# Top-k attention and an MLP on one core: GpSimd's sums in two set places of a step, with a third buffer, and earlier copies in the last two steps

## The chip, the core and the metric

The kernel runs on one core of a Trainium2 chip. A core has five engines that run side by side, each through its own list of instructions in order: TensorE (PE, matmuls; PEld is its loading of weights), VectorE (DVE), ScalarE (ACT), GpSimd (POOL) and SyncE (SP, which here only issues DMAs). They wait for each other through semaphores. The metric is the device time of one launch in microseconds (us); lower is better.

## The reference, cut to what matters

```python
def _attn_ref(q, k, v):                       # 8 batches, 8 heads, 576 rows, 64 columns
    scores = np.matmul(q, k.transpose(0, 1, 3, 2)) / np.sqrt(D)
    kth = np.partition(scores, -32, axis=-1)[..., -32:-31]
    scores = np.where(scores >= kth, scores, -1e9)
    scores = scores - np.max(scores, axis=-1, keepdims=True)
    attn = np.exp(scores)
    attn = attn / (np.sum(attn, axis=-1, keepdims=True) + 1e-09)
    return np.matmul(attn, v)

def _moe_ref(x, w_in, w_out):                 # x 4608x512, w_in 512x2048, w_out 2048x512
    h = x @ w_in
    neg, pos = h <= -1.0, h >= 1.0
    g = np.where(pos, h, np.where(neg, 0.0, (h + 1.0) ** 2 / 4.0))
    return g @ w_out
```

Between the two, the attention output of all heads of a row becomes one row of `x`. So each row of scores keeps its 32 largest entries, and the MLP's activation is zero, a parabola or the identity.

## The kernel before

**Steps and chunks.** The attention is done in 144 steps (`steps`), each with two tiles of 128 rows of scores with 576 columns. Four steps give the 128 rows of `x` of one chunk; there are 36 chunks, and `mlp` puts the MLP of a chunk into a list, `pending`, as soon as its attention is done.

**VectorE in a step.** `weights` finds the 32nd largest of each row. `pairs` (L381) makes `more` and `less`, the larger and the smaller of columns j and j+288. MAX8 takes eight largest entries at a time, and MATCH_REPLACE8 (L388) removes them. A scan (L460) merges the two lists into the threshold `kth`, and L467 multiplies `e`, the exponentials, by the mask, and sums them up. VectorE then takes the reciprocal `rz` (L413).

**Dividing and turning the weights.** `divide` has GpSimd multiply `e` by `rz` (L420, two instructions a step, and a small one, `excess`, L423). `move_w` has ScalarE copy `e` into two halves of 16 bits (`halves`, L497, one buffer), SP write them to DRAM (`rows`), and SP read them back transposed into `wT` by a DMA (L296), issued in a later place through `reads_of_rows`. `values` multiplies `wT` by v on TensorE (`po`, L514 and L522), and ScalarE copies the result into `xT`. In the first eight steps, while weights of the MLP are still converted (`early`), TensorE transposes instead and the halves aren't used.

**The MLP of a chunk.** `hidden` multiplies a group of 256 hidden units (`ph`, L547; 8 groups a chunk). `read` has ScalarE make `r` and `g` from it (L558, L566). `bound` has GpSimd bound `r` to at most 1, square it, and add it to `g` (L573, L575, L576): these are GpSimd's sums. `final` multiplies 128 hidden units of `g` by `w_out` into `py` (L586). The finals of a group are listed four groups (`LAG`) behind its `hidden`. After the last final, ScalarE copies `py`, which has one buffer, to `y` (L589). The very last chunk is cut finer, takes its sums on VectorE, and has its finals in halves (`py_half`, L600).

**The order of the work.** It is written out by hand: all engines run in the order in which the main loop emits. A step m has seven slots. In slot 0 `weights` emits two MAX8 with `divide` of step m-1, and two MATCH_REPLACE8; in slot 1 two more of each; in slot 3 `more` of step m+1, `less` of step m, and the first MAX8 of step m+1 with its first `exp`; in slot 4 the second `exp`; in slot 5 the rest, up to L467. `move_w` of step m-1 stands in slot 3. In slot 2 of every even step stand the scores (`sp`, L367) of two steps and the `values` of two. In each slot, `advance` emits as much of `pending` as the estimated TensorE time allows.

**GpSimd's sums before.** `read` appends a `bound` to the list `bounds`, with the number of the slot. It is emitted when the next `read` finds more than one in the list, when a final needs it, or at the end of the slot two or more after its own. `r` has two buffers, so ScalarE's read of a group waits until the sums of the group two before it are done.

Of the kernel before, what the change touches and what calls it, by code (L numbers as in the profile page):

```python
# [11 lines left out]
F32 = mybir.dt.float32  # L12
# [5 lines left out]
ALU = mybir.AluOpType  # L18
# [8 lines left out]
def kernel(  # L27
# [10 lines left out]
    nc = tc.nc  # L38
    B, H, S, D = q.shape
    NTOK, DM = out.shape  # L40
    DFF = moe_w_in.shape[1]
    P = 128
# [8 lines left out]
    SH = S // 2  # L51
# [4 lines left out]
    GROUP = 2  # L56
# [120 lines left out]
    def run(ctx, paired):  # L177
# [197 lines left out]

        def pairs(st, op, name, bufs):
            s = st["s"]
            st[name] = x = att.tile([P, 2, SH], F32, name=name, bufs=bufs)  # L380
            nc.vector.tensor_tensor(out=x, in0=s[:, :, 0:SH], in1=s[:, :, SH:S], op=op)  # L381

        def largest(st, r):
            return [partial(nc.vector.max, out=eight(st["tops"], i, r), in_=st["rest"][:, i, :]) for i in range(2)]
# [6 lines left out]
        def first_top(st, between=None):  # L391
            s, e = st["s"], st["e"]
            if paired:
                pairs(st, ALU.max, "more", 2)
            if between is not None and paired:
                pairs(between, ALU.min, "less", 1)
            st["rest"] = st["more"] if paired else s
            st["tops"] = tops = att.tile([P, 2 * TOP_K], F32, name="tops", bufs=3)
            nmax = att.tile([P, 2], F32, name="nmax")
            for x in largest(st, 0):  # L400
                x()  # L401
            nc.scalar.activation(nmax, tops[:, 0:2 * SPLIT:SPLIT], AF.Copy, scale=-1.0)
            for i in range(2):
                nc.scalar.activation(e[:, i, :], s[:, i, :], AF.Exp, bias=nmax[:, i:i + 1])  # L404
                yield
# [132 lines left out]
        def mlp(xT, rows, pool, last):  # L538
            gs, group, whole_g = {}, 1 if last else GROUP, set()
            py = []  # L540

            def hidden(x):
                ph = ps.tile([P, group, P], F32, name="ph", tag="ph", bufs=3)
                for i in range(group):
                    f = x * group + i
                    for kk in range(NK):
                        nc.tensor.matmul(ph[:, i], w_in[:, kk, f * P:(f + 1) * P], xT[:, kk],  # L547
                                         start=(kk == 0), stop=(kk == NK - 1))

                reads.append(partial(read, x, ph))  # L550
                if not holding:
                    issue_reads()

            def read(x, ph):
                while len(bounds) > 1:
                    bounds.popleft()[1]()
                r = pool.tile([P, GROUP, P], F32, name="r", bufs=2)[:, 0:group]
                nc.scalar.activation(r, ph, AF.Relu, bias=half, scale=0.5 * unit)  # L558
                gs[x] = g = pool.tile([P, GROUP, P], F32, name="g", bufs=2 * LAG)[:, 0:group]
                if last:  # L560
                    nc.scalar.activation(g, ph, AF.Relu, bias=minus_half, scale=0.5 * unit)
                    nc.vector.scalar_tensor_tensor(out=r, in0=r, scalar=1.0, in1=r, op0=ALU.min, op1=ALU.mult)
                    nc.vector.tensor_tensor(out=g, in0=r, in1=g, op=ALU.add)
                    whole_g.add(x)
                    return
                nc.scalar.activation(g, ph, AF.Relu, bias=minus, scale=unit)  # L566
                by_act = converted < n_pieces and x % 2
                if by_act:
                    nc.scalar.activation(r, r, AF.Square)
                bounds.append((slots_done, partial(bound, x, r, g, by_act)))  # L570

            def bound(x, r, g, by_act):
                nc.gpsimd.tensor_scalar(r, r, 1.0, 0.0, ALU.min, ALU.max)  # L573
                if not by_act:
                    nc.gpsimd.tensor_tensor(out=r, in0=r, in1=r, op=ALU.mult)  # L575
                nc.gpsimd.tensor_tensor(out=g, in0=r, in1=g, op=ALU.add)  # L576
                whole_g.add(x)

            def final(f):
                if f == 0:  # L580
                    py.append(ps.tile([P, DM], F32, name="py", tag="py", bufs=1))
                if f // group not in gs:
                    issue_reads()
                while f // group not in whole_g:
                    bounds.popleft()[1]()
                nc.tensor.matmul(py[0], gs[f // group][:, f % group], w_out[:, f, :], start=(f == 0), stop=(f == NF - 1))  # L586
                if f == NF - 1:
                    y = (late or words).tile([P, DM], F32, name="y", bufs=1)
                    nc.scalar.activation(y, py[0], AF.Copy, scale=unit)  # L589
                    for p0, p1, dst in rows:  # L590
                        nc.sync.dma_start(out=dst, in_=y[p0:p1])

            HALF = DM // 2

            def final_half(f, c):
                if f == 0:
                    py.append(ps.tile([P, HALF], F32, name="py_half", tag="a" if c else "py", bufs=2 if c else 1))
                nc.tensor.matmul(py[c], gs[f][:, 0], w_out[:, f, c * HALF:(c + 1) * HALF], start=(f == 0), stop=(f == NF - 1))  # L600

            def final_halves(f):
                for c in range(2):
                    final_half(f, c)

            def last_finals():
                for c in range(2):
                    for f in range(NF - LAG, NF):
                        final_half(f, c)
                    y = late.tile([P, HALF], F32, name="y_half", tag="y", bufs=1) if c else \  # L610
                        pool.tile([P, HALF], F32, name="y_first", tag="r", bufs=2)
                    nc.scalar.activation(y, py[c], AF.Copy, scale=unit)
                    for p0, p1, dst in rows:
                        nc.sync.dma_start(out=dst[:, c * HALF:(c + 1) * HALF], in_=y[p0:p1])

            behind = []
            while pending and pending[-1][3]:
                behind.insert(0, pending.pop())
            for x in range(NF // group + LAG):
                if last and x == 0:  # L620
                    for _ in range(2):
                        pending.append(behind.pop(0)[0:3] + (False,))
                if x < NF // group:
                    pending.append((NK * group, needed(x * group + group - 1, False), partial(hidden, x), False))
                if x < LAG:
                    for _ in range(min(GROUP + 1, len(behind))):
                        pending.append(behind.pop(0)[0:3] + (False,))
                elif last:
                    if x < NF:
                        pending.append((DM // P, needed(x - LAG, True), partial(final_halves, x - LAG), True))  # L630
                    elif x == NF:
                        pending.append((LAG * DM // P, needed(NF - 1, True), partial(last_finals), True))
                else:
                    for f in range((x - LAG) * group, (x - LAG + 1) * group):
                        pending.append((DM // P, needed(f, True), partial(final, f), x >= NF // group))
# [14 lines left out]
        n = len(steps)  # L650
# [8 lines left out]
        converted, inspected, due = 0, 0, 0.0  # L659

        reads, bounds, holding, slots_done = [], deque(), False, 0

        def issue_reads():
            while reads:
                reads.pop(0)()
# [75 lines left out]
        state = []  # L741
# [41 lines left out]
        for _ in first_top(state[0]):  # L783
            pass
# [19 lines left out]
        for m in range(n + 2):  # L804
            early = converted < n_pieces
# [21 lines left out]
            for slot in range(SLOTS):  # L827
# [11 lines left out]
                if slot == 1 and 1 <= m <= n and state[m - 1]["by_tensor"]:  # L839
                    pe_time = max(pe_time, done[m - 1] + 2.0) + 1.0  # L840
                    transpose_w(state[m - 1])
                    ready_at[m - 1] = pe_time + 1.8
                if slot == 3 and 1 <= m <= n and state[m - 1] is not None and not state[m - 1]["by_tensor"]:
                    move_w(state[m - 1])
                    ready_at[m - 1] = done[m - 1] + 15.0
                if slot == 1 and late is not None and paired and m % 2 == 0:
# [47 lines left out]
                        nc.tensor.transpose(rest[:, i % NT, :], ident, ident)  # L894
                advance((EARLY_SHARE if early else share) / SLOTS if m < n - 2 else 32.0, now)
                slots_done += 1
                while bounds and (early or m >= n or bounds[0][0] < slots_done - 2):
                    bounds.popleft()[1]()
            for _ in (top_k if top_k is not None else ()):
                pass  # L900
        while pending:
            advance(32.0, pe_time + 8.0)
            while bounds:
                bounds.popleft()[1]()
        order.__exit__(None, None, None)


# [45 lines left out]
```

## Time and profile before

| what | before |
|---|---|
| median of 3 runs | 1471.42 us (1471.32 to 1472.72) |
| the profiled execution | 1469.45 us, of which span 1467.6 |
| PE busy | 1430.7 us (97%) |
| DVE busy | 1396.8 us (95%) |
| ACT busy | 1161.1 us (79%) |
| POOL busy | 928.5 us (63%) |
| chain that ended last | PE 78%, DVE 14%, ACT 4%, DMA 2%, issue 2% |

A span goes from the first to the last instruction. Busy time is the union of an engine's instructions. The chain that ended last is followed back from the last instruction to whatever released it, step by step. A group of instructions is named by its line, engine and operation, and by what it writes and reads. A wait is idle time of an engine just before an instruction, and is put down to what came last.

### The profile page before, as it was taken

Reading aid. Unit: us, or ns where it says so; the run is one execution under the profiler, and the core shown is the slowest. Engines: PE = TensorE matmul, PEld = TensorE weight load, DVE = VectorE, ACT = ScalarE, POOL = GpSimd, SP = SyncE. Lnnn points to the kernel's source line nnn. Section 1 sums busy time; section 2 is a strip of 40 time slices with the busy share of each in tenths; the row PEclk is TensorE's granted clock in tenths of the full one; section 3 lists DMA queues with packets and bytes.
Section 4 is the critical chain, followed back from the end, with each engine's and each line's share of the span. In section 5 each row is a group of like instructions: output and inputs, shape, how many; then the busy total and the mean of one; then the engine's idle time right before and its main releaser. Section 6 shows DMA issues by size and latency. Waiting matters only on the chain.

```text
span 1467.6 us, 31975 instructions
## 1 busy us (share of the span) xinstructions
PE 1430.7 (97%) x10731; PEld 1045.9 (71%) x10731; DVE 1396.8 (95%) x4392; ACT 1161.1 (79%) x2216; POOL 928.5 (63%) x1314
## 2 busy tenths in 40 slices
PE   7998899999999999999999999999999999999998
PEld 5766577777777777777777777777777777777677
DVE  6989999999999999999999999999999999999932
ACT  6986878888778888887778887888778888777643
POOL 3473576667666666666666666666666666676640
PEclk7999999999999999999999999999999999999999
DMA  7642767886668886987667986887668886665430
GB/s 240 194 133 64 189 180 196 218 206 172 173 171 212 217 206 178 221 216 178 167 172 201 216 213 173 219 225 184 159 168 199 218 212 175 171 172 153 137 105 18
DMA packets 517919, 264.87 MB, mean 180 GB/s; under 512 B 467696, under 2 KB 476144, under 8 KB 517744
## 3 DMA queue, kind: packets, MB, share of 16 engines
q1 hardware_dynamic: 517744, 262.73, 68.3%
q8 instruction: 87, 1.43, 0.4%
q14 instruction: 88, 0.72, 0.2%
HBM read 62.39 MB, written 104.86 MB: 114 GB/s over the span
## 4 chain that ended last, share of the span: by engine, by line
PE 78%; DVE 14%; ACT 4%; DMA 2%; issue 2%; SPq 0%; ACTq 0%
PE ph L547 29%; PE py L586 27%; PE sp L367 9%; PE po L514 8%; DVE more L388 3%; DVE e L467 3%; DVE more L381 1%; DVE less L381 1%; DVE tops L429 1%; DVE tops L437 1%; PE pw L482 1%; DVE tops L448 1%; DVE seconds L455 1%; PE po L522 1%; PE py_half L600 1%
## 5 line engine op out<-in xcount | busy, mean ns | idle before, releaser
L547 PEld LDWEIGHTS ph<-xT,w_in 128*128 128x128 f32 x4608 | 547.7, 192 | 97.8 <-issue 66.4
L547 PE MATMUL ph<-xT,w_in 128*128 128x128 f32 x4608 | 556.3, 276 | 2.7 <-ACT g L566 2.1
L586 PE MATMUL py<-w_out,g 128*128 128x512 f32 x1120 | 527.0, 598 | 2.0 <-ACT y L589 2.0
L573 POOL TENSOR_SCALAR r<-r 128x256 f32<-128x256 f32 x280 | 136.2, 487 | 398.2 <-ACT r L558 394.0
L388 DVE MATCH_REPLACE8 more<-tops,more 128x288 f32<-128x288 f32 x864 | 374.7, 437 | 0.0
L420 POOL TENSOR_SCALAR e<-e,rz 128x576 f32<-128x576 f32 x272 | 307.7, 1141 | 11.9 <-DVE rz L413 11.9
L586 PEld LDWEIGHTS py<-w_out,g 128*128 128x128 f32 x1120 | 194.2, 191 | 166.0 <-issue 164.7
L497 ACT COPY halves<-e 128x1152 uint16<-128x1152 uint16 x272 | 297.8, 1142 | 2.0 <-DMA rows<-halves 2.0
L576 POOL TENSOR_TENSOR g<-r,g 128x256 f32<-128x256 f32 x280 | 229.8, 821 | 22.0
L467 DVE SCALAR_TENSOR_TENSOR e<-s,kth,e 128x577 f32<-128x577 f32 x288 | 241.0, 872 | 0.1
L404 ACT ACTIVATE e<-s,nmax 128x576 f32<-128x576 f32 x288 | 222.5, 773 | 4.7
L558 ACT ACTIVATE r<-ph,half 128x256 f32<-128x256 f32 (+1 forms) x296 | 136.6, 462 | 99.5 <-PE ph L547 88.3
L368 ACT ACTIVATE s<-sp 128x576 f32<-128x576 f32 x288 | 171.9, 650 | 37.3 <-PE sp L367 34.6
L575 POOL TENSOR_TENSOR r<-r 128x256 f32<-128x256 f32 x276 | 180.2, 653 | 23.0
L367 PE MATMUL sp<-kT,qT 64*128 64x288 f32 x1024 | 163.1, 436 | 4.8 <-ACT kT L265 3.4
L514 PE MATMUL po<-wT,v_in 128*64 128x128 f32 x2048 | 139.1, 277 | 6.5 <-DMA wT<-rows 6.2
L367 PEld LDWEIGHTS sp<-kT,qT 64*128 64x128 f32 x1024 | 90.3, 189 | 76.2 <-issue 30.8
L381 DVE TENSOR_TENSOR more<-s 128x576 f32<-128x576 f32 x144 | 136.1, 945 | 7.9 <-ACT s L368 7.9
L514 PEld LDWEIGHTS po<-wT,v_in 128*64 128x64 f32 x2048 | 113.9, 137 | 31.7 <-issue 13.0
L566 ACT ACTIVATE g<-ph,minus 128x256 f32<-128x256 f32 x280 | 130.8, 467 | 0.0
L429 DVE MAX8 tops<-more 128x8 f32<-128x288 f32 x288 | 125.3, 442 | 0.0
L401 DVE MAX8 tops<-more 128x8 f32<-128x288 f32 x288 | 116.2, 442 | 0.0
(95 smaller groups left out, 1340.8 us busy)
## 6 DMA issues: line engine op xcount, KB each, us to landing
rows<-halves SPq DMA_DIRECT2D x136, 576.0 KB, 3.2
lines<-parts SPq DMA_DIRECT2D x52, 256.0 KB, 3.4
q_in<-in_q_dram SPq DMA_DIRECT2D x32, 256.0 KB, 4.0
v_in<-in_v_dram SPq DMA_DIRECT2D x32, 256.0 KB, 3.9
raw<-in_moe_w_in_dram SPq DMA_DIRECT2D x32, 256.0 KB, 3.4
raw<-in_moe_w_out_dram SPq DMA_DIRECT2D x32, 256.0 KB, 3.4
out_dram<-y SPq DMA_DIRECT2D x31, 256.0 KB, 3.3
kT<-in_moe_w_in_dram SPq DMA_DIRECT2D x8, 512.0 KB, 4.8
```

Source lines behind the costliest of these rows:

```text
L367: nc.tensor.matmul(*x, start=True, stop=True)
L368: nc.scalar.activation(s[:, :, c0:c1], sp[:, :, 0:SH], AF.Copy, scale=SCALE)
L388: nc.vector.match_replace(out=st["rest"][:, i, :], in_to_replace=eight(st["tops"], i, r - 8), in_values=src[:, i, :], imm_value=LOWEST)
L404: nc.scalar.activation(e[:, i, :], s[:, i, :], AF.Exp, bias=nmax[:, i:i + 1])
L420: nc.gpsimd.tensor_scalar(st["e"][:, i, :], st["e"][:, i, :], rz[:, i:i + 1], 1.0, ALU.mult, ALU.mult)
L467: nc.vector.scalar_tensor_tensor(out=st["all"][1][:, i, :], in0=st["all"][0][:, i, :], scalar=last[i], in1=st["all"][1][:, i, :], op0=ALU. ...
L497: nc.scalar.copy(halves[:, :, i * S:(i + 1) * S], st["e"][:, i, :].bitcast(U16).rearrange("p (k t) -> p t k", t=2))
L514: nc.tensor.matmul(po[j * D:(j + 1) * D], v_in[:, h, c, :] if c < NT else tail_values(v_tl, h, t), wT[:, block(j, c)], start=(c == 0), sto ...
L547: nc.tensor.matmul(ph[:, i], w_in[:, kk, f * P:(f + 1) * P], xT[:, kk], start=(kk == 0), stop=(kk == NK - 1))
L575: nc.gpsimd.tensor_tensor(out=r, in0=r, in1=r, op=ALU.mult)
L576: nc.gpsimd.tensor_tensor(out=g, in0=r, in1=g, op=ALU.add)
L586: nc.tensor.matmul(py[0], gs[f // group][:, f % group], w_out[:, f, :], start=(f == 0), stop=(f == NF - 1))
```

## The change

It does four things. `r` gets a third buffer, and `read` empties `bounds` only when more than two groups stand in it. The three operations of a group become single entries, so that part of a group can be emitted. After the conversion, and before the attention ends, they are emitted in two places: two at the end of slot 0, four at the end of slot 3, and the first of the four waits until VectorE has done `less` (the result of `pairs`, kept in `pairs_done`). And `move_w` stands in slot 1 instead of 3 for the last step but one, and in slot 0 for the last.

```diff
+        pairs_done = None
+
         def pairs(st, op, name, bufs):
...
-            nc.vector.tensor_tensor(out=x, in0=s[:, :, 0:SH], in1=s[:, :, SH:S], op=op)
+            return nc.vector.tensor_tensor(out=x, in0=s[:, :, 0:SH], in1=s[:, :, SH:S], op=op)
...
             if between is not None and paired:
-                pairs(between, ALU.min, "less", 1)
+                nonlocal pairs_done
+                pairs_done = pairs(between, ALU.min, "less", 1)
...
             def read(x, ph):
-                while len(bounds) > 1:
-                    bounds.popleft()[1]()
-                r = pool.tile([P, GROUP, P], F32, name="r", bufs=2)[:, 0:group]
+                while len(bounds) > 2:
+                    bound_some(len(bounds[0]))
+                r = pool.tile([P, GROUP, P], F32, name="r", bufs=3)[:, 0:group]
...
-                bounds.append((slots_done, partial(bound, x, r, g, by_act)))
-
-            def bound(x, r, g, by_act):
-                nc.gpsimd.tensor_scalar(r, r, 1.0, 0.0, ALU.min, ALU.max)
+                work = [partial(nc.gpsimd.tensor_scalar, r, r, 1.0, 0.0, ALU.min, ALU.max)]
                 if not by_act:
-                    nc.gpsimd.tensor_tensor(out=r, in0=r, in1=r, op=ALU.mult)
-                nc.gpsimd.tensor_tensor(out=g, in0=r, in1=g, op=ALU.add)
-                whole_g.add(x)
+                    work.append(partial(nc.gpsimd.tensor_tensor, out=r, in0=r, in1=r, op=ALU.mult))
+
+                def complete():
+                    whole_g.add(x)
+                    return nc.gpsimd.tensor_tensor(out=g, in0=r, in1=g, op=ALU.add)
+
+                work.append(complete)
+                bounds.append(work)
...
                 while f // group not in whole_g:
-                    bounds.popleft()[1]()
+                    bound_some(1)
...
+        def bound_some(amount, behind=None):
+            for _ in range(amount):
+                if not bounds:
+                    break
+                ins = bounds[0].pop(0)()
+                if behind is not None:
+                    tc.add_manual_dep(getattr(ins, "ins", ins), getattr(behind, "ins", behind).name,
+                                      mybir.DependencyInfo(mybir.DependencyClass.Sync, mybir.DependencyReason.ANTI),
+                                      reason="GpSimd's sums stand between VectorE's")
+                    behind = None
+                if not bounds[0]:
+                    bounds.popleft()
...
-                if slot == 3 and 1 <= m <= n and state[m - 1] is not None and not state[m - 1]["by_tensor"]:
+                if slot == (3 if m < n - 1 else n - m) and 1 <= m <= n and state[m - 1] is not None and not state[m - 1]["by_tensor"]:
                     move_w(state[m - 1])
...
                 slots_done += 1
-                while bounds and (early or m >= n or bounds[0][0] < slots_done - 2):
-                    bounds.popleft()[1]()
+                if early or m >= n:
+                    while bounds:
+                        bound_some(1)
+                elif slot == 0:
+                    bound_some(2)
+                elif slot == 3:
+                    bound_some(4, pairs_done)
```

More of the change, by code (lines that the diff above doesn't have):

```diff
@@ L610, in last_finals @@
                     y = late.tile([P, HALF], F32, name="y_half", tag="y", bufs=1) if c else \
-                        pool.tile([P, HALF], F32, name="y_first", tag="r", bufs=2)
+                        pool.tile([P, HALF], F32, name="y_first", tag="r", bufs=3)
                     nc.scalar.activation(y, py[c], AF.Copy, scale=unit)
@@ L903, in run @@
             while bounds:
-                bounds.popleft()[1]()
+                bound_some(1)
         order.__exit__(None, None, None)
```

## The prediction

> **What bounds the kernel now.** I read the page's first two parts, then the table of busy time by stretch, the waits by stretch, the chain of waits, and last the timeline of single engines where those pointed.
>
> The stretches (window, length, then busy us of PE, PEld, DVE, ACT, POOL, the granted clock, DMA share, GB/s):
>
> ```profile
> 182.00:430.00 248.00, 245.23 (x1876) 178.68 (x1877) 248.00 (x782) 200.46 (x384) 165.27 (x230) 1.00 0.72 188
> 430.00:1384.00 954.00, 954.00 (x7237) 693.07 (x7234) 954.00 (x3027) 781.79 (x1480) 647.55 (x913) 1.00 0.74 191
> 1384.00:1421.50 37.50, 37.50 (x259) 26.89 (x257) 22.80 (x70) 20.15 (x37) 24.58 (x41) 1.00 0.46 132
> 1421.50:1430.50 9.00, 6.11 (x46) 4.23 (x46) 0.45 (x2) 0.53 (x2) 0.07 (x1) 0.81 0.32 66
> ```
>
> Two engines are full at once from 430 to 1384, so busy time does not decide. Start-to-start times do. In the TensorE timeline between 805 and 823 us each run begins where the last one's issue ends: 16 `ph` matmuls take 1.79 us, 4 `py` matmuls 1.72 us, and these numbers recur in every period of four steps (37.77 us). No TensorE wait at all is listed between 440 and 1390. VectorE's durations do vary there. In this group table for 440 to 1390 (busy us, mean ns, idle before) the unequal pair is `more` and `less`, the same operation on the same shape:
>
> ```profile
> L467 DVE SCALAR_TENSOR_TENSOR e<-s,kth,e 128x577 f32<-128x577 f32 x202 | 164.4, 849 | 0.0
> L381 DVE TENSOR_TENSOR more<-s 128x576 f32<-128x576 f32 x100 | 97.5, 975 | 0.0
> ...
> L381 DVE TENSOR_TENSOR less<-s 128x576 f32<-128x576 f32 x100 | 74.5, 745 | 0.0
> ```
>
> and on GpSimd's side:
>
> ```profile
> L420 POOL TENSOR_SCALAR e<-e,rz 128x576 f32<-128x576 f32 x200 | 241.6, 1217 | 0.0
> ```
>
> `more` costs 0.23 us more than `less`; L467's shortest is 801 ns against a mean of 849; L420's shortest is 737 against 1217. The two engines block each other. So from 430 on TensorE sets the pace and VectorE's lost time is its slack. Before that it is VectorE: the chain from 380 to 424 us is nearly all DVE, and TensorE waits:
>
> ```profile
> PE py L586 <- ACT y L589: 2.0, 4, 1.3
> PE po L522 <- ACT s L368: 0.6, 1, 0.6
> PE po L514 <- DMA wT<-rows: 0.2, 1, 0.2
> ```
>
> At the end TensorE stands still once more, and restarts slowly (the 40 `po` before took 2.33 us, these last 20 take 2.33 alone):
>
> ```profile
> 1418.11 3.60 PE L586 MATMUL py<-w_out,g 128*128 128x512 f32 x8
> 1421.64 1.09 PE L514 MATMUL po<-wT,v_in 128*64 128x128 f32 x16
> 1422.56 0.39 PE L514 MATMUL po<-wT,v_tail 128*64 128x128 f32 x4
> 1425.84 1.98 PE L514 MATMUL po<-wT,v_in 128*64 128x128 f32 x16 [2.89 <-DMA wT<-rows]
> 1427.54 0.70 PE L514 MATMUL po<-wT,v_tail 128*64 128x128 f32 x4
> 1428.17 0.37 PE L915 MATMUL pworst<-ident,worst 128*1 128x128 f32 x1
> 1428.34 2.36 PE L586 MATMUL py<-w_out,g 128*128 128x512 f32 x4
> 1430.53 1.05 PE L547 MATMUL ph<-xT,w_in 128*128 128x128 f32 x8
> ```
>
> **What the skill says.** The Trainium skill, "SBUF — State Buffer", section "Who interferes with whom": a VectorE operation with two SBUF inputs contends with a GpSimd operation that reads SBUF; the first holds the port for its whole instruction and the other waits; with one input VectorE does not contend. The trace agrees: `more`, `less` and L467 have two inputs and stretch, MAX8 and MATCH_REPLACE8 have one and stay within some ns of 436. "TensorE: Matmul & The Clock Gate", section "What's actually happening": TensorE falls to half clock after idling and needs sustained work to return. The trace agrees at the end: granted clock 0.81 and doubled spacing after the pause at 1423. "Perfetto Trace Analysis", section "Tensor Engine Instruction (MATMUL, LD_WEIGHTS)": matmul ends are a model, which is why I use start to start.
>
> **The change, part by part.**
>
> *GpSimd's sums.* Nothing is added to or removed from any engine but a wait; two groups a step, three operations each, are still six a step, and the change places 2+4. The waiting instruction is the first of the four sums, behind `less`. Queued behind it: the other three sums, and then the next step's two L420; ACT waits for those through `halves`, and for `r` buffers, TensorE for `g`. I check each with the steps whose `rz` start at 764.57 and 774.14.
>
> (a) Slot 0. `rz` ends at 774.28; two L420 at 0.74 each, 0.17 for `excess`, then `r` min 0.48 and square 0.61 end near 777.1. `more` starts at 776.98. All between are one-input operations, so the overlap left is 0.1 to 0.2 us.
> (b) Slot 3. `less` of the first step starts at 768.31, and its successor at 768.98. Four sums of 0.70, 0.48, 0.69 and 0.70 (start to start) end near 771.6; L467 starts at 772.09. They fit.
> (c) So VectorE's step loses about 0.23 + 2x0.05 = 0.33 us of blocking and keeps 0.1 to 0.2: 9.44 becomes some 9.25 us. TensorE's 37.77 per four steps (9.44) does not move. From 430 to 1384 I count nothing: the cover is TensorE's own work.
> (d) Latest reader. Walking the queue, groups read by ACT in a period come to 2, 1, 2, 3 per step and leave no remainder. Tightest: the group read at 767.80 gets min and square in the next step's slot 0, its addition after that step's `less` (778.72), so near 779.5; TensorE's eight `py` from 780.35 need it at the third final, 782.1. Margin 2.5 us. The third `r` buffer frees each at least 4 us ahead of its next writer. Cost nothing; if `less` comes over 2.5 us later against TensorE, a stall per chunk.
> (e) 182 to 430. TensorE's delayed starts there, beyond regular spacing: 1.51 at 195.17, 0.46 at 233.34, 0.85 at 255.64, 0.34 at 293.88, 0.47 at 386.42, 0.48 at 424.67, together 4.1 us. Most is the single `py` waiting for ACT's `y`, which stands behind `exp` and `halves`, and these wait for VectorE. VectorE's blocking in this stretch is 0.41 us a step (`more` 860, `less` 800, L467 919 against 741, 741 and 801), over 26 steps far more than needed, but the stall at 195 comes too soon to go whole. Bounds 0 and 4.1; I take 3.0. What is late next is TensorE.
> (f) Before 182: until 115 the sums are emitted at once in both versions. The stalls from 137 to 161 hang on a chain of ACT copies and two DMAs (`halves` 151.37, `rows` 153.58, `wT` 156.80 to 161.38) that no sum enters. I take 0; -2 to +1.5, since VectorE is full there too.
>
> *The last two steps.* `rz` of the step before last is at 1397.93, but its L420 starts at 1402.08 behind one group of sums; its `halves` only at 1409.00, behind five reads, of which one waited 3.42 us for an `r` buffer. The last step's `rz` is at 1405.82, its L420 at 1411.96 behind three more groups, its `halves` at 1415.14 after 2.04 us of waiting for the single `halves` buffer, still being read by the DMA. Then 2.21 + DMA near 3.2 + transposing DMA 4.69 give 1425.8.
> After: the sums held back let L420 follow `rz` at once, so 1398 to 1399.5, and `halves` in place 1 comes after about three reads, near 1403; its `rows` DMA issues at 1405.5 and lands near 1409. SP's queue takes the `wT` transpose next and then the last `rows`; the `y` write at 1403.87 is short. Last step: L420 behind the four sums of slot 3 and one group that a read flushes, near 1407; `halves` in place 0, ahead of the `xT` copies, near 1409 to 1411; `rows` 1411.3 to 1414.5; `wT` to 1419.2. TensorE asks at 1422.8. Margin 3.6 us, so the wait goes whole. ACT's reads and `xT` copies move back by one or two 2.2 us copies; `ph` has three buffers and the matmuls of 1406.79 need the read of 1402.13, so I charge nothing, at most 1 us.
> Without the wait `po` 1.17, the transpose 0.2 and `py` 1.75 end at 1425.9 instead of 1430.53: 4.6 us, with the slow clock in it. I take 4.5 (bounds 2.5 and 4.8). From there the last chunk runs on TensorE unchanged.
>
> **Sum.** 3.0 + 0 + 4.5 = 7.5 us. The profiled execution took 1469.45 (span 1467.6): it would take 1462.0. The median of the runs is 1.97 us higher, 1471.42, so 1463.9.
>
> **Rivals.**
> A (forecast, 0.62): as above, 1460.5 to 1466.
> B, only the tail or only the middle pays (0.15): 4.5 or 3.0 off, 1466.9 or 1468.4. For it: VectorE is full from 137 to 430, so the `y` waits may shift to another order. Against: they vanish by themselves in the old kernel after 430.
> C, no change (0.07): VectorE's slack is refilled by new collisions and the last `halves` still comes late behind flushed sums; 1470 to 1471.4.
> D, slower (0.10): the four sums that wait for `less` reach the third final of the eight `py` too late. It decides once `less` falls more than 2.5 us back against TensorE. At 0.5 us for each of some 33 chunks that is 16.5 us, less the 4.5 of the tail: 1483. For it: one strict queue with a cross-engine wait. Against: margins in (d), and VectorE gets faster, not slower.
> E, larger gain (0.06): the stalls before 182 shrink too, another 2 to 4 us: 1460.
> That the placing fails to separate the engines would be C; (a) and (b) speak against it.
>
> **The numbers.** Likeliest 1463.9. The range 1459 to 1469.5 takes in A, E and nearly all of B; D, C and scraps of the others stay out. What a measurement here can tell from no change is about 0.2%, 2.9 us, so faster means below 1468.5: A, E and most of B, 0.82. Within 0.2%: C and B's rest, 0.08. Slower: 0.10.
>
> **What would show it.** Mean `more` near 0.80 or below and L420 near 0.75; L467 near 0.81; VectorE with idle time before `more` or on `s` after 430; still no TensorE wait there and the period still 37.77; no `y` waits of TensorE after 233; L420 within 0.2 us behind `rz`; the last `po` without a DMA wait, and the last chunk's first `ph` still 37 us before the end of the span but some 7 us sooner than 1430.5. **What would make it wrong:** a TensorE wait on a GpSimd `g` between 440 and 1390, a changed period, or a last `wT` that lands after TensorE asks.

## The result, and the profile after

The median fell from 1471.42 to 1466.79 us (9 runs each; the changed kernel's lie between 1464.32 and 1468.83). The ratio of the two kernels' times is 0.9965, with a 95% interval of 0.9954 to 0.9975. That is about 5.2 us faster (the medians alone lie 4.6 us apart), where 7.5 were forecast. Each ratio below is to runs of the kernel before that were made alongside, whose median lay between 1469.95 and 1471.42 us, so the ratios can be compared more closely than the times. The profiled execution took 1464.38 us, 5.07 less than that of before.

The page's span and busy times of the changed kernel:

```profile
span 1462.1 us, 32172 instructions
...
PE 1426.9 (98%) x10731; PEld 1043.3 (71%) x10731; DVE 1392.5 (95%) x4392; ACT 1159.5 (79%) x2216; POOL 810.1 (55%) x1314
```

GpSimd was busy 118 us less with the same 1314 instructions: its multiplications no longer wait inside, as the lines below show. VectorE's share has not moved. The stretches (columns as before the change):

```profile
182.00:430.00 248.00, 247.01 (x1893) 180.26 (x1892) 248.00 (x789) 203.12 (x389) 141.56 (x235) 1.00 0.75 189
430.00:1384.00 954.00, 953.57 (x7234) 692.74 (x7233) 954.00 (x3027) 781.07 (x1481) 551.68 (x909) 1.00 0.76 191
...
1384.00:1421.00 37.00, 36.61 (x255) 25.77 (x255) 18.21 (x56) 16.89 (x33) 23.86 (x39) 1.00 0.48 136
1421.00:1426.00 5.00, 5.00 (x50) 3.67 (x47) 0.45 (x2) 0.67 (x3) 0.00 (x0) 1.00 0.00 2
```

The stretch around 1421 has no idle time and full clock now. Two places before it, each under half a microsecond, are new: 0.43 us of idle TensorE between 430 and 1384, and 0.39 from 1384 on. TensorE's waits from 182 to 1430 us name them:

```profile
PE po L525 <- DMA wT<-rows: 0.7, 1, 0.7
PE sp L367 <- ACT s L368: 0.4, 1, 0.4
PE py L591 <- POOL g L579: 0.4, 1, 0.4
PE po L517 <- DMA wT<-rows: 0.3, 1, 0.3
```

The four waits for `y` are gone from this profile. In the VectorE groups from 440 to 1390 us the old inequality is gone too:

```profile
L470 DVE SCALAR_TENSOR_TENSOR e<-s,kth,e 128x577 f32<-128x577 f32 x200 | 162.7, 848 | 0.0
...
L383 DVE TENSOR_TENSOR less<-s 128x576 f32<-128x576 f32 x101 | 77.1, 763 | 0.0
L383 DVE TENSOR_TENSOR more<-s 128x576 f32<-128x576 f32 x101 | 76.3, 755 | 0.0
...
L463 DVE TENSOR_TENSOR_SCAN kth<-tops,seconds 128x25 f32<-128x25 f32 x100 | 40.0, 400 | 0.0
```

and of GpSimd:

```profile
L423 POOL TENSOR_SCALAR e<-e,rz 128x576 f32<-128x576 f32 x201 | 148.4, 749 | 227.7 <-DVE rz L416 227.7
```

`more` fell from 975 to 755 ns, and GpSimd's multiplication (now L423) from 1217 to 749. But L470, the old L467, kept its 848, and the threshold scan doubled. Before, it was

```profile
L460 DVE TENSOR_TENSOR_SCAN kth<-tops,seconds 128x25 f32<-128x25 f32 x101 | 19.7, 195 | 0.0
```

The end, in the TensorE timeline:

```profile
1417.03 3.60 PE L591 MATMUL py<-w_out,g 128*128 128x512 f32 x8
1420.55 1.09 PE L517 MATMUL po<-wT,v_in 128*64 128x128 f32 x16
1421.48 0.39 PE L517 MATMUL po<-wT,v_tail 128*64 128x128 f32 x4
1421.70 1.04 PE L517 MATMUL po<-wT,v_in 128*64 128x128 f32 x16
1422.57 0.39 PE L517 MATMUL po<-wT,v_tail 128*64 128x128 f32 x4
1422.89 0.27 PE L938 MATMUL pworst<-ident,worst 128*1 128x128 f32 x1
1423.00 1.88 PE L591 MATMUL py<-w_out,g 128*128 128x512 f32 x4
1424.71 1.05 PE L550 MATMUL ph<-xT,w_in 128*128 128x128 f32 x8
```

The last chunk's first `ph` comes at 1424.71 instead of 1430.53.

**A common ruler.** All these kernels give TensorE the same 10731 matmuls in the same order. So the start of the n-th matmul can be compared between two profiles, and the difference, taken at the matmuls that began at 200, 430, 1384, 1421 and 1432 us in the first profile of before, tells in which stretch time came or went. The first column is the difference reached at 200 us, the others are what each stretch added; us, negative is sooner.

```
profile                          at 200  200-430  430-1384  1384-1421  1421-1432
before, second profile             1.49     0.85      1.14       0.00      -1.55
changed                           -1.23    -1.21      0.65       0.70      -4.74
changed, second profile           -0.94    -1.39      0.30       0.42      -4.73
places and buffer, old copies     -0.88    -1.16     -0.11       0.41      -4.54
buffer and copies, no places      -0.78    -0.14      0.38       0.00      -4.74
earlier copies alone              -0.40     1.02      0.13       0.00      -4.73
third buffer alone                 0.99    -1.12      0.50       0.00      -4.54
```

The first column depends on the execution: over the first 182 us the two profiles of the changed kernel differ by 3.6 us (0.28 and -3.28 at 182), so nothing below rests on the start.

Up to the last two steps several of these kernels are the same program, so their rows repeat each other there. From 200 to 430 us the old placing with two buffers gives 0 (the first profile itself), 0.85 and 1.02; the third buffer without the places -0.14 and -1.12; the places with the third buffer -1.21, -1.39 and -1.16. So a single entry of that column is good to about 1 us.

### The profile page after: what moved, and what is told of

Same layout as the page of the kernel before. It is cut to its first block, busy times and chain, and to the rows that moved or that the text cites. A ratio compares the mean times of both kernels' runs of the same rounds, so it can differ in the third digit from the quotient of the medians.

```text
span 1462.1 us, 32172 instructions
## 1 busy us (share of the span) xinstructions
PE 1426.9 (98%) x10731; PEld 1043.3 (71%) x10731; DVE 1392.5 (95%) x4392; ACT 1159.5 (79%) x2216; POOL 810.1 (55%) x1314
## 4 chain that ended last, share of the span: by engine, by line
PE 77%; DVE 13%; ACT 4%; DMA 3%; issue 2%; SPq 1%; POOL 1%; POOLq 0%; ACTq 0%
PE ph L550 29%; PE py L591 27%; PE sp L367 9%; PE po L517 8%; DVE more L390 3%; DVE e L470 2%; PE pw L485 1%; DVE more L383 1%; DVE tops L432 1%; DVE tops L440 1%; DMA wT<-rows 1%; DVE less L383 1%; PE po L525 1%; PE py_half L605 1%; DVE tops L451 1%
## 5 line engine op out<-in xcount | busy, mean ns | idle before, releaser
L423 POOL TENSOR_SCALAR e<-e,rz 128x576 f32<-128x576 f32 x272 | 201.9, 753 | 308.3 <-DVE rz L416 308.3
L579 POOL TENSOR_TENSOR g<-r,g 128x256 f32<-128x256 f32 x280 | 207.4, 741 | 125.7 <-DVE less L383 89.3
L470 DVE SCALAR_TENSOR_TENSOR e<-s,kth,e 128x577 f32<-128x577 f32 x288 | 235.4, 852 | 0.1
L672 POOL TENSOR_SCALAR r<-r 128x256 f32<-128x256 f32 x280 | 144.8, 517 | 115.9 <-ACT r L561 111.2
L672 POOL TENSOR_TENSOR r<-r 128x256 f32<-128x256 f32 x276 | 187.5, 679 | 22.8
L383 DVE TENSOR_TENSOR more<-s 128x576 f32<-128x576 f32 x144 | 111.0, 771 | 7.7 <-ACT s L368 7.7
```

Of the source, the lines that this page charges most:

```text
L423: nc.gpsimd.tensor_scalar(st["e"][:, i, :], st["e"][:, i, :], rz[:, i:i + 1], 1.0, ALU.mult, ALU.mult)
L470: nc.vector.scalar_tensor_tensor(out=st["all"][1][:, i, :], in0=st["all"][0][:, i, :], scalar=last[i], in1=st["all"][1][:, i, :], op0=ALU. ...
L579: return nc.gpsimd.tensor_tensor(out=g, in0=r, in1=g, op=ALU.add)
L672: ins = bounds[0].pop(0)()
```

## The experiments

**Earlier copies alone.** The kernel before with one line changed.

```diff
-                if slot == 3 and 1 <= m <= n and ...
+                if slot == (3 if m < n - 1 else n - m) and 1 <= m <= n and ...
```

> The kernel before with only the earlier copies in the last two steps. Theory (the places matter: GpSimd's multiplications L420 of the last two steps come late behind sums, so that earlier copies alone have to wait for them): the last multiplication still ends near 1413.4, copies 2.2 us, row DMA 3.2, transpose 4.7 give 1423.5, so the DMA wait of the last products shrinks from 2.9 to about 0.7 us and the time by 2 to 4 us, about 1468. The waits of TensorE for y before 430 us stay. Rival (the tail gain comes from the copies alone): the wait goes whole, 4.5 us or more, 1466.9 or below.

Measured: 1465.91 us, ratio 0.9970 (0.9959 to 0.9981). The tail went whole, 4.73 us, as the rival had it. The theory's times were right and its conclusion was not. The last multiplication did start late (1412.80), the last copy waited 1.76 us for it, and its row DMA was issued at 1415.81 against 1417.67 before. But the transpose could issue 2.84 us after that, the two DMAs together were done by the 7.7 us at which TensorE asked, and the copy before the last no longer held the buffer. ScalarE's timeline:

```profile
1403.60 2.21 ACT L497 COPY halves<-e 128x1152 uint16<-128x1152 uint16 x2 [0.26 <-POOL e L420]
...
1413.58 2.21 ACT L497 COPY halves<-e 128x1152 uint16<-128x1152 uint16 x2 [1.76 <-POOL e L420]
```

**Places and buffer, old copies.** The changed kernel with that line as it was.

> The changed kernel with the copies of the last two steps back in slot 3. Theory: TensorE's waits for y before 430 us are gone as in the changed kernel, worth 2.7 us there; of the tail a part comes too, since the last multiplication no longer stands behind sums, but the copy stands behind the copies of xT, near 1412 to 1413 instead of 1415: 1.5 to 3 us of the 4.6. Together about 1468.5 to 1470. Rival (the places are worth nothing, all is the copies): 1471.

Measured: 1465.05 us, 0.9966 (0.9955 to 0.9978). Faster than expected: the tail went nearly whole here as well (4.54). The last copy stood at 1411.24, and its transpose was issued at 1416.41, 4.6 us sooner than in the old kernel. As this execution was already 1.75 us ahead at 1421, that is 2.9 us sooner for TensorE.

**Third buffer alone.**

```diff
-                while len(bounds) > 1:
+                while len(bounds) > 2:
...
-                r = pool.tile([P, GROUP, P], F32, name="r", bufs=2)[:, 0:group]
+                r = pool.tile([P, GROUP, P], F32, name="r", bufs=3)[:, 0:group]
...
-                        pool.tile([P, HALF], F32, name="y_first", tag="r", bufs=2)
+                        pool.tile([P, HALF], F32, name="y_first", tag="r", bufs=3)
```

> The kernel before with the third r buffer and the list emptied above two groups, the old placing by age. Theory (the separation of the two engines makes the middle's gain, and the buffer alone only lets ScalarE run on): more stays near 0.97 us and the waits for y before 430 us stay within 1 us of the old; tail gains at most 1 us from reads that wait less; 1470 to 1471.5. Rival (the buffer is what pays): waits for y gone and 1468.5 or below.

Measured: 1466.18 us, 0.9969 (0.9956 to 0.9982). `more` stayed at 972 ns, as expected, but again the tail went nearly whole (4.54): with less waiting for buffers ScalarE reached the copies at 1407.10 and 1413.37. The kernel before had them at

```profile
1409.00 2.20 ACT L497 COPY halves<-e 128x1152 uint16<-128x1152 uint16 x2
1415.14 2.21 ACT L497 COPY halves<-e 128x1152 uint16<-128x1152 uint16 x2 [2.04 <-DMA rows<-halves]
```

So the earlier copies alone and the third buffer alone each remove the DMA wait at the end; the tail of the buffer alone is 0.2 us short of the full gain. The transpose came 2.9 us too late, and against TensorE it is issued 3.1 us sooner with the earlier copies and 2.9 us with the buffer. The two do not add: both together, without the places, take no more off the tail (4.74) than the copies alone (4.73). What the places do at the end is not shown. No run had them without the buffer and without the earlier copies, and with the buffer they moved the transpose no further (2.9 us) than the buffer alone.

**Without the wait for `less`.**

```diff
-                    bound_some(4, pairs_done)
+                    bound_some(4)
```

> The changed kernel without the wait of the four sums for less. Theory (from 182 us on TensorE sets the pace, and what GpSimd takes from VectorE is VectorE's slack): sums collide with more and less again, more back above 0.85 us on the mean, but the time within 1 us of the changed kernel, 1466 to 1468, and the waits for y before 430 us at most partly back. Rival (the wait is what makes the gain): 1469 or more.

Measured: 1492.73 us, 1.0151 (1.0131 to 1.0171). The theory fell. From 430 to 1384 this kernel lost 19.4 us against the first profile of before, and TensorE waits for ScalarE there:

```profile
PE po L517 <- ACT g L569: 12.0, 19, 1.0
```

The VectorE groups show why:

```profile
L470 DVE SCALAR_TENSOR_TENSOR e<-s,kth,e 128x577 f32<-128x577 f32 x196 | 151.5, 808 | 0.0
L383 DVE TENSOR_TENSOR less<-s 128x576 f32<-128x576 f32 x98 | 124.4, 1270 | 0.0
...
L383 DVE TENSOR_TENSOR more<-s 128x576 f32<-128x576 f32 x98 | 72.8, 743 | 0.0
```

In each of the 98 steps an addition of GpSimd's starts 0.48 to 0.50 us ahead of `less`, and `less`, which takes 0.74 us unblocked, loses 0.53 us to it. I had treated what GpSimd takes as slack without asking how much slack there is. It can be worked out: VectorE's start-to-start times above those of an unblocked instruction, summed over a step from 440 to 1390, are the time in which it was blocked. As VectorE shows no idle time there, this blocking is also all that its step holds beyond its own work.

```
us a step, 440 to 1390     more   less   scan   L467/L470   sum     step
before                     0.23   0.00   0.00   0.09       0.321   9.452
changed                    0.01   0.02   0.20   0.09       0.319   9.455
without the wait           0.00   0.53   0.00   0.01       0.530   9.666
small pad (below)          0.01   0.01   0.02   0.09       0.132   9.479
large pad (below)          0.00   0.00   0.00   0.01       0.022   9.847
```

Step less blocking is 9.13 us in the first three rows. TensorE needs 9.45, so VectorE can lose 0.32 us a step; 0.53 is 0.21 too much, and 0.21 us in 98 steps is 20.6 us, near the measured 19.4.

**A pad on VectorE.** One more MAX8 with one input in each step (0.21 us), or two (288 and 144 columns), on the changed kernel; the results are unused.

```diff
+                spare = att.tile([P, 8], F32, name="spare", bufs=1)
+                for width in (144,):
+                    nc.vector.max(out=spare, in_=st["less"][:, 0, 0:width])
```

> The changed kernel with one more VectorE operation of one input in every step, MAX8 over 144 columns, some 0.21 us, its result unused. Theory (TensorE paces the stretch 430 to 1384 at 9.44 us a step, VectorE needs only 9.11 unblocked, and fills the difference with being blocked): the stretch stays within 1 us of the changed kernel's, and VectorE's blocking, now about 0.33 us a step, falls by about 0.2. Rival (VectorE, busy all the time, paces): 0.21 x 101 steps = 21 us more in that stretch.

> The changed kernel with two such operations, 288 and 144 columns, some 0.57 us a step. Theory: 9.11 + 0.57 = 9.68 us exceeds TensorE's 9.44 by 0.24, so 24 us more between 430 and 1384 if no blocking is left, up to 35 if some is; in all 1495 to 1510. Rival (VectorE paces): 0.57 x 101 = 58 us more in that stretch.

Measured, small: 1467.99 us, 0.9985 (0.9976 to 0.9993) against the kernel before. From 430 to 1384 it was 0.49 us slower than the changed kernel, not 21, and the blocking fell by 0.187 us a step, nearly the pad. The whole run still costs about 3 us more than the changed kernel by the two ratios. Its profile puts the loss before 430, where VectorE paces: between 182 and 200 us it fell back by 6.1 us against the changed kernel. But that execution was the slowest of its 20 (1473.18), and part of the 6.1 is a restart of TensorE at half clock, so the size is not settled. Large: 1523.47 us; 36.6 us more than the changed kernel from 430 to 1384, above the expected 24 to 35, because the pair took 9.847 - 0.022 - 9.136 = 0.69 us a step and not 0.57 (the first of the two alone takes 0.48 us start to start). The blocking is all but gone, and VectorE paces. Both speak for the theory: from 430 to 1384 a VectorE that is 100% busy was not the bound, and its blocked time is where its slack lies.

**Two buffers with the places.**

```diff
-                while len(bounds) > 2:
+                while len(bounds) > 1:
...
-                r = pool.tile([P, GROUP, P], F32, name="r", bufs=3)[:, 0:group]
+                r = pool.tile([P, GROUP, P], F32, name="r", bufs=2)[:, 0:group]
...
-                        pool.tile([P, HALF], F32, name="y_first", tag="r", bufs=3)
+                        pool.tile([P, HALF], F32, name="y_first", tag="r", bufs=2)
```

> The changed kernel with the old two r buffers, and the list emptied above one group. Theory (the list of up to two groups and the third buffer are what lets sums wait for their places): with two buffers a read empties the list at once, so most sums are emitted outside the two places and more or less is blocked again, near 0.85 us on the mean; the tail gain stays (earlier copies alone give it): 1466 to 1472, with up to 4 us lost between 182 and 1384. Rival (the buffer is not needed once the places are set): as the changed kernel, within 1 us in every stretch.

Measured: 1467.39 us, 0.9975 (0.9966 to 0.9985), an interval that overlaps the changed kernel's. `more` and `less` are blocked again (958 and 885 ns), as expected: without the third buffer the places are not kept. Its profile shows 6.5 us lost from 430 to 1421, of which TensorE waited 3.2 us for GpSimd's `g`; but that execution was the slowest of its 14 (1471.99), so the price is not settled.

**Copies in slot 1 of every step.**

```diff
-                if slot == (3 if m < n - 1 else n - m) and 1 <= m <= n and ...
+                if slot == (1 if m < n else 0) and 1 <= m <= n and ...
```

> The changed kernel with the copies into halves in slot 1 of every step (slot 0 for the last), two places earlier than slot 3. Theory (TensorE's waits for wT at 161, 254 and 292 us, 3.9, 0.9 and 0.5 us in the changed kernel, hang on when the copies stand in ScalarE's queue, and the multiplications no longer come late): these waits go, with the slow clock behind the first, 3 to 6 us: 1461 to 1464. Rival (the copies now push back scores and reads on ScalarE, which TensorE waits for): no gain or a loss, 1467 to 1475.

Measured: 1512.62 us, 1.0285 (1.0258 to 1.0311). The rival was right, at a higher price than it named. Waits from 182 to 1400:

```profile
ACT halves L500 <- DMA rows<-halves: 79.8, 30, 6.8
...
PE sp L367 <- ACT s L368: 27.6, 10, 4.0
```

ScalarE reaches the copy before the row DMA has emptied the single `halves` buffer, and everything behind it on ScalarE waits, scores among it.

**No places: third buffer and earlier copies.**

> The changed kernel without the two places: the kernel before with the third buffer, the list emptied above two, and the earlier copies. Theory now (the tail's 4.6 us need only one of the three parts, and the places give 1 to 2 us before 430 us, most of it handed back later): 1465 to 1467, within 1.5 us of the changed kernel, more still blocked at 0.97 us. Rival (the places are worth the middle's 2.7 us and nothing is handed back): 2.5 us or more above the changed kernel.

Measured: 1464.09 us (5 runs), 0.9968 (0.9955 to 0.9980), against 0.9965 (0.9954 to 0.9975) with the places. `more` was at 976 ns. Taking the places out of the changed kernel costs nothing that can be measured; with intervals this wide, a difference of some 2 us would not show.

**Sums at once in the last two steps.**

```diff
-                if early or m >= n:
+                if early or m >= n - 2:
```

> The changed kernel with sums emitted at the end of every slot already in the last two steps of the attention. Theory (the 0.70 us that the changed kernel loses between 1384 and 1421 is the held-back sum that py waits for at 1390): that stretch shortens by 0.5 to 0.7 us and the last copies keep enough margin, so the tail stays; 0.5 us in all, too little for the ratio. Rival (the last multiplications then come late again): 2 to 4 us lost at the tail.

Measured: 1466.22 us, 0.9975 (0.9968 to 0.9982). The theory was wrong, and the rival half right: the stretch from 1384 to 1421 was 0.87 us longer than before, where the changed kernel had 0.70. The last multiplications did come late again (the last at 1412.48, not 1405.51), but the tail still gained 3.89 of 4.7, with a DMA wait of 0.6 us back. The sums ahead of that `py` stand in the same order as in the changed kernel. Every profile with the places loses 0.41 us or more in this stretch, but for the one with copies in slot 1 of every step, and all those that keep placing by age lose 0.00. In the changed kernel GpSimd stood still for 2.49 us, waiting for `rz`, before the six sums ahead of that `py`. Two of these collided with `more` and `less` and were stretched to 1.15 and 0.90 us, and the last, an addition, ended at 1390.65. In the kernel before, the same addition ended at 1390.31, but TensorE reached the `py` that needs it only at 1391.89 and did not wait. So TensorE's lead met sums that came no sooner. That accounts for the wait of 0.39 us; the rest of the 0.70 is open.

**Second profiles.**

> The kernel before, a second profile. Theory: its start differs from the first by up to 3 us at 182 us (arrival of the first DMAs), but from 430 to 1384 and in the tail it repeats the first within 0.3 us, with the tail's DMA wait.

> The changed kernel, a second profile. Theory: start differs as above; no wait for y before 430 us; the losses of 0.65 us between 430 and 700 and of 0.70 between 1384 and 1421 come again; no DMA wait in the tail.

The kernel before did not repeat within 0.3 us. From 430 to 1384 it had a wait of 1.0 us for ScalarE's `xT` that the first lacked. At the end it waited as long as the first, and yet its tail was 1.55 us shorter:

```profile
1426.04 0.39 PE L514 MATMUL po<-wT,v_tail 128*64 128x128 f32 x4
1429.39 1.09 PE L514 MATMUL po<-wT,v_in 128*64 128x128 f32 x16 [2.96 <-DMA wT<-rows]
1430.29 0.42 PE L514 MATMUL po<-wT,v_tail 128*64 128x128 f32 x4
...
1430.74 1.88 PE L586 MATMUL py<-w_out,g 128*128 128x512 f32 x4
```

The `po` after the pause take 1.09 and 0.42 us, not 1.98 and 0.70: the granted clock stayed full this time, where the first profile has 3.41 us at half clock. Of the changed kernel's 4.74 us at the end, then, 1.55 are the slow clock, which not every execution of the kernel before pays. The changed kernel's second profile repeated the tail and part of the losses (0.30 and 0.42). TensorE's wait for `y`, absent from the first, was back:

```profile
PE py L591 <- ACT y L594: 2.0, 1, 2.0
PE po L525 <- DMA wT<-rows: 1.0, 1, 1.0
```

## Why the prediction was right in sign and range, and 2.3 us too large

**What bounds the kernel** held. TensorE paces from 430 to 1384 us; the pads show it from VectorE's side.

**(a) and (b), the separation,** held for `more`, `less` and GpSimd's multiplications. (b) overlooked an operation: between `less` and L467 stands the scan, which has two inputs too. The last of the four sums ends near 771.6 by (b)'s own times, and the scan begins at 771.56 in that step. It was blocked by 0.20 us a step in the changed kernel: in all 100 steps it began inside one of GpSimd's sums and ended 64 to 72 ns behind it. So L467 did not fall to the 0.81 us that was forecast, either.

**(c)** was right that the stretch gains nothing, and wrong about VectorE. It forecast a step of some 9.25 us and idle time. The step stayed at 9.455, without idle time, and the blocking went from 0.321 to 0.319 us. The separation moved the blocking to other operations and did not lower it. What VectorE did gain was distance: counted by the start of each step's `rz`, it was 4.05 us sooner than before at 430 and 4.26 at 1384, while TensorE was 2.44 and 1.79 sooner (5.12 and 4.78 against 2.33 and 2.03 in the second profile). So it ran further ahead of TensorE and then kept its distance. That GpSimd's sums, which come when ScalarE's reads allow it, are what stops VectorE there fits the blocked scans, but no run changed only when these sums come. From 190 to 440, where VectorE did pace, the blocking fell from 0.41 to 0.32 (0.43 and 0.45 in the repeats of before, 0.32 in those with the places; 0.33 and 0.41 with the buffer and no places).

**(d)** held for the steady stretch: no TensorE wait for `g` between 430 and 1384. It did not hold at 1390 (0.39 us), just behind the window that the prediction named as its sign of being wrong. And the rival D, a loss through the wait for `less`, had it the wrong way round: without that wait the changed kernel is some 27 us slower (1.0151 against 0.9965).

**(e)** is one term that was mis-sized. It took 3.0 of 4.1 us from 182 to 430. The first pair of profiles comes near it, with 1.52 us gained up to 200 and 1.21 from there on. But the first of these is not the change's for good: the wait at 195, 1.5 us of the 4.1, is back in the second profile with 2.0 us, after a start that was 3.6 us sooner. At 200 the two profiles of the changed kernel are within 0.3 us of each other, so VectorE's chain sets that point and not TensorE's. From 200 on the two gained 1.21 and 1.39, or about 1.9 against the mean of the three profiles with the old placing.

**What (d) charged at nothing** is the other: 0.70 and 0.42 us from 1384 to 1421, where no profile with the old placing shows any. The 0.65 and 0.30 us from 430 to 1384 can't be laid to the change, since the second profile of the kernel before shows 1.14 there.

**The tail** was right in size, 4.5 forecast and 4.74 and 4.73 measured, against a first profile that paid for the slow clock. The way there went as described: the last two multiplications started at 1394.02 and 1405.51, the copies at 1401.40 and 1408.48, the last transpose at 1414.92. Its reason was too narrow. Sums held back, earlier reads and earlier copies were told as one chain, when the earlier reads or the earlier copies alone are enough. One sum of it is off, too: 2.21, 3.2 and 4.69 us from 1415.14 give 1425.2 and not 1425.8, because the gap of 0.3 us between copy and row DMA and the full 3.35 us to the transpose's issue are needed to get there.

**The sum from 200 us on** is -4.6 and -5.4 us in the two profiles of the changed kernel, and +0.4 in the second of the kernel before, which agrees with the ratio (5.2 us). Of this the places can claim at most some 2 us before 430, shared with the buffer in a way that the profiles do not tell apart, and hand back about half a microsecond at 1384. The ratios agree: without the places 0.9968, with the earlier copies alone 0.9970, with the buffer alone 0.9969, all within each other's intervals. What is surely faster is the end, and one line would have done it.

## What to carry to other kernels

An engine that is busy all the time may still not be the bound: if its durations stretch by waiting for a shared port, the slack lies inside them, and a pad of known length on it tells in one run whether there is as much as that. Separating two engines that collide paid nothing here where the one that is blocked did not set the pace. And when a change has several parts that act on the same chain, try each alone, since a wait of 3 us can be removed only once, and try them also from the other side, each taken out of the whole.

## What the runs showed of the hardware that was not expected

A scan of only 25 columns lost as much to GpSimd as an operation of 576 columns does: it went from 195 to 400 ns on the mean, and `more` had lost 230. That fits what the Trainium skill, "SBUF — State Buffer", section "Who interferes with whom", says of the port pair that VectorE and GpSimd share: it is an exclusive lock, and who issues first has it for the whole instruction (said there of VectorE's two-port mode; of operations with two inputs, that they contend). The traces show it here for operations with two inputs. The scan ended 64 to 72 ns behind GpSimd's instruction in all 100 steps of the changed kernel, and without the wait for `less`, `less` ended 0.61 to 0.62 us behind GpSimd's addition in 96 of 98. So the loss depends on what is left of the other engine's instruction and not on one's own length.

And after pauses of 2.89 and 2.96 us TensorE came back once at half the pace and once at full pace. Other profiles here add pauses near 195 us: 1.97 us (places and buffer, old copies), 1.99 (changed, second profile), 2.14 (sums at once in the last two steps) and 2.77 (third buffer alone) were each followed by 3.41 us at half clock, and one of 2.06 (earlier copies alone) by none. So in this kernel a TensorE wait of some 2 us can cost some 1.7 us more (an estimate: half of 3.41), and whether it does differs from run to run.
